# An attention and MLP kernel: token chunks of 512 in place of 384, and the PSUM banks shared out anew

## The chip, the cores and the metric

The kernel runs on one core of one Trainium2 chip. The core has TensorE (PE, matrix products; PEld is its loading of the stationary operand), VectorE (DVE), ScalarE (ACT), GpSimd (POOL) and SyncE (SP), which issues the DMAs. The metric is the device time of one execution in microseconds. Sums of matmuls land in PSUM, which has eight banks of 128 partitions x 512 float32.

## What is computed

Attention over 8 batches, 8 heads, 576 tokens and 64 dimensions a head, with two masks, and then a block over the 512 dimensions of the joined heads:

```
scores = where(mask[h], q @ k.T / 8, -1e9)    # 32 tokens back, or every 4th of 128 back
attn   = exp(scores - max) / (sum + 1e-9)
x      = (attn @ v) joined over heads         # 8 x 576 x 512
u      = x + (x.T @ U @ V).T                  # U: 576 x 32, V: 32 x 576, over the tokens
out    = u + relu(u @ w_ch1) @ w_ch2          # 512 -> 2048 -> 512
```

U and V mix all the tokens of a batch, so no token of a batch can enter the last line before the attention of its whole batch is done. The 8 x 576 = 4608 tokens are 36 tiles of 128.

## The kernel before

**The MLP.** It works on chunks of CT = 3 tiles (384 tokens), 12 chunks. A chunk has 16 steps f, one for each 128 of the 2048 hidden values. Step f of layer 1 (`layer1`) sums 12 matmuls of 384 columns in one PSUM bank (tile `ph`): each product is made of a high and a low part of both operands, as w1h x uth, w1l x uth, w1h x utl, four matmuls each. ACT then writes the high part of the relu (`hh`, L751), and DVE the low part (`hl`, L752), which reads both `ph` and `hh`. Step f of layer 2 (`layer2`) adds, for each token tile, hh x w2h, hh x w2l and hl x w2h, 512 columns each, to the tile's bank (`acc`). At the end of a chunk DVE adds `acc` to x (L788) and SP stores it. The transposed high and low parts of the chunk's tokens, `uth` (ACT, L579) and `utl` (DVE, L580), are made before the chunk begins, from a tile transposed on PE (tiles 0 to 5) or by DVE and DMA (`turn_x`, from tile 6 on).

**The banks.** Three serve attention and the rest (`ps`), three hold `acc`, two hold `ph`.

**Attention.** A batch has nine groups of four units. A unit is a score matmul (`s`), an addition of the mask (L407) and the negated row maximum (L410, `nmax`) on DVE, the exponential on ACT (L414). DVE transposes the group's result in 32 x 32 blocks (L440, L443, eight instructions), PE multiplies by v (`pv`), and DVE normalizes and writes x (L479). From batch 2 on a score's operands are split in a high and a low part first, by ACT (L354) and POOL (L355, L358). When a batch is done, x is multiplied by U (`t`, L519), split (`ts`), multiplied by V (`m`, L543) and added to x (L545).

**What sets the order.** Batch 0 runs first, and in it the weights begin: each piece is read as int64 words and narrowed by ACT, DVE (L210, L214) and POOL, then split (L222, L223). The rest of the weights is emitted through the steps of chunk 0 (`weight_step`, W_RATE a step). The items of batches 1 to 7 stand in a list (`queue`) with a position in chunks; `slot()`, called between groups of the MLP's matmuls, emits the items whose position has come. Batch b runs from position 1.5b - 2.1 to 1.5b - 0.8 (384-token chunks); batch 1 is done at 0.55. What the program emits is put into each engine's order by a scheduler at build time; the engines run their orders as they stand.

Of the kernel before, what the change touches and what calls it, by code (L numbers as in the profile page):

```python
# [10 lines left out]
F32 = mybir.dt.float32  # L11
# [21 lines left out]
HALF_D = DM // 2  # L33
FC = DF // P
NTILE = B * S // P
CT = 3
CTOK = CT * P
NCHUNK = NTILE // CT
UNITS = 4
# [6 lines left out]
NGB = len(TILES) // 2  # L46
# [1 line left out]
DPART = [[NJ - 1]] + [[j, j + 1] for j in range(0, NJ - 1, 2)]  # L48
NU = 9 + len(DPART)
LAG = 2  # L50
MARGIN = 0.3
PRE_AT = range(1, 7)
PRE_N = 6
W_FROM = 11
W_EACH = 3
W_RATE = 4
# [91 lines left out]
def attention_moe_kernel(ctx: ExitStack, tc: tile.TileContext, qk1, qk2, vv, masks, wide, ident, ut, vt, w1, w2, out):  # L148
# [217 lines left out]
    def score(g, u):  # L366
        n = UNITS * g + u
        two = n >= N2 and not is_odd(n)
        if u == 0:
            p_sb = work.tile([P, UNITS, KW], F32, tag="p", name=f"p{g}", bufs=2)  # L370
            pool, n_ = (early, 3) if g < NGB else (work, 2)
            nmax = pool.tile([P, UNITS], F32, tag="nmax", name=f"nmax{g}", bufs=n_)
            ssum = pool.tile([P, UNITS], F32, tag="ssum", name=f"ssum{g}", bufs=n_)
            state[g] = [p_sb, nmax, ssum, None]
        if two:
            sp = psum.tile([P, 2 * KW], F32, tag="ps", name=f"s{g}_{u}")
            split_qk(n)
            t = pairs.pop(n)
            nc.tensor.matmul(sp, lhsT=t[:, 0:P], rhs=t[:, P:], start=True, stop=True)  # L379
# [42 lines left out]
    def turn(g, p_sb):  # L422
        pt = pts[g % NPT]
        if g < PE_T:
            tp = psum.tile([KB, UNITS, P], F32, tag="ph" if g < NGB else "ps", name=f"ptp{g}", bufs=2 if g < NGB else 3)
            for u in range(UNITS):
                nc.tensor.transpose(out=tp[:, u, :], in_=p_sb[:, u, 0:KB], identity=id_sb)
            if g in PT_ACT:
                nc.scalar.copy(out=pt, in_=tp)
            else:  # L430
                nc.vector.tensor_copy(out=pt, in_=tp)  # L431
            return pt
        for r in range(P // WIN):
            rs = slice(WIN * r, WIN * (r + 1))
            for k in (r % 2, r % 2 + 1):
                ks = slice(WIN * k, WIN * (k + 1))
                if is_wide(g):
                    s = r // 2
                    to = pt[ks, 2 * s:2 * s + 2].rearrange("k p (h q) -> k (p h) q", h=2)
                    nc.vector.transpose(out=to[:, :, WIN * (r % 2):WIN * (r % 2 + 1)],  # L440
                                        in_=p_sb[rs, :, QB * s + WIN * k:QB * s + WIN * (k + 1)])
# [45 lines left out]
    t_ps = {}  # L487
# [94 lines left out]
    def batch_items(b):  # L582
# [47 lines left out]
        after = []  # L630
        for c in range(2):
            more = []
            for i in range(n + 1):
                def go(i=i, c=c):
                    if i > 0:
                        t_mm(b, i - 1, c)
# [79 lines left out]
    for b in range(1, B):  # L716
        lo, hi = max(0.0, 1.5 * b - 2 - LO0), 1.5 * b - 0.5
        if b == 1:
            hi = HI1
        its = batch_items(b)  # L720
        queue += [(lo + (hi - MARGIN - lo) * at_, it) for at_, it in its]
    for t in range(DVE_FROM * CT, NTILE):
        done = 1.5 * ((P * t + P - 1) // S) - 0.5 - MARGIN
        at_ = max(t // CT - 1 + TURN_AT + TURN_GAP * (t % CT), done)
        queue.append((at_, lambda t=t: turn_x(t)))
    queue.sort(key=lambda e: e[0])

    for c in range(NCHUNK):
        slots = [0]
        uh, ul = uts.pop(c)  # L730
        acc = [psum.tile([P, DM], F32, tag="acc", name=f"acc{c}_{i}", bufs=3) for i in range(CT)]
        ht = {}

        def slot():
            pos = c + slots[0] / (6 * FC - 3)
# [133 lines left out]
```

## Time and profile before

| | us |
|---|---|
| median of three runs | 1045.84 |
| lowest, highest | 1044.07, 1045.98 |
| the profiled execution | 1044.13 |
| its span, first to last instruction | 1042.3 |

The mean granted clock of PE over the span is 0.972. The page's busy times overlap each other. Rows of instruction groups give the line, engine and operation, output <- input, the count, the busy time, the mean ns of one and the idle time ahead of it. Matmuls are pipelined and their ends are modelled, so what a matmul costs is read from start to start in the timeline. A float32 matmul stands as two rows.

### The profile page before, as it was taken

What the parts mean: (1) busy time and instruction counts of PE and PEld (TensorE: products, weight loads), DVE (VectorE), ACT (ScalarE), POOL (GpSimd) and SP (SyncE); (2) the same over time, 40 slices, a digit from 0 to 9 for tenths busy, and PEclk for the clock granted to TensorE, in tenths of its full rate; (3) what the DMA queues carried; (4) which work ended last, traced back from release to release, by engine and by line L of the source; (5) the groups of instructions that cost most, each with busy time, mean ns of one, the idle gap of its engine ahead of it and who ended that gap; (6) DMA issues with size and microseconds to landing.
All of it is one profiled execution on the core that took longest, in us unless ns stands there. A gap on an engine that the chain in (4) does not pass through costs nothing.

```text
span 1042.3 us, 17400 instructions
## 1 busy us (share of the span) xinstructions
PE 997.2 (96%) x5304; PEld 895.1 (86%) x5304; DVE 669.3 (64%) x2238; ACT 411.3 (39%) x1225; POOL 338.4 (32%) x533
## 2 busy tenths in 40 slices
PE   6679888999999999999999999999999999999997
PEld 6568776898899898999889898999889898999996
DVE  5999998776557863777547873777737874311211
ACT  4646744445233632544324542445324542111110
POOL 1568756434122621425213431325214431000000
PEclk9669899899999999999999999999999999999999
DMA  9656724433232422424232431524233320500000
GB/s 278 190 178 202 234 91 119 111 103 97 73 90 83 127 82 74 117 82 126 82 82 79 120 96 45 138 78 125 74 91 90 104 75 26 130 1 1 31 1 31
DMA packets 97198, 103.06 MB, mean 99 GB/s; under 512 B 12848, under 2 KB 84080, under 8 KB 97104
## 3 DMA queue, kind: packets, MB, share of 16 engines
q1 hardware_dynamic: 97104, 101.94, 34.0%
q8 instruction: 43, 0.70, 0.3%
q14 instruction: 51, 0.42, 0.1%
HBM read 79.86 MB, written 17.30 MB: 93 GB/s over the span
## 4 chain that ended last, share of the span: by engine, by line
PE 81%; DVE 12%; DMA 3%; issue 2%; ACT 1%; SPq 0%; POOL 0%; DVEq 0%; ACTq 0%; POOLq 0%
PE ph L746 36%; PE acc L763 35%; PE pv L451 5%; PE s L379 3%; DVE v L214 2%; PE t L519 2%; DVE pt L443 2%; DVE v L210 1%; DVE utl L580 1%; PE m L543 1%; DMA raw<-ut 1%; DMA raw<-w 1%; DMA raw<-vt 1%; PE s L390 1%; DVE hl L752 1%
## 5 line engine op out<-in xcount | busy, mean ns | idle before, releaser
L763 PE MATMUL acc<-w2h,hh 128*128 128x512 f32 x576 | 229.0, 398 | 4.5 <-ACT hh L751 4.5
L763 PE MATMUL acc<-w2l,hh 128*128 128x512 f32 x576 | 228.1, 396 | 0.0
L355 POOL TENSOR_TENSOR qks<-qkr,qks 128x160 fp32r<-128x160 f32 x192 | 104.1, 542 | 375.4 <-ACT qks L354 262.8
L763 PE MATMUL acc<-w2h,hl 128*128 128x512 f32 x576 | 214.2, 399 | 4.5 <-DVE hl L752 4.4
L752 DVE SCALAR_TENSOR_TENSOR hl<-ph,hh 128x384 fp32r<-128x384 f32 x192 | 105.9, 552 | 166.4 <-ACT hh L751 166.0
L751 ACT ACTIVATE hh<-ph 128x384 fp32r<-128x384 f32 x192 | 93.5, 487 | 280.5 <-PE ph L746 270.7
L414 ACT ACTIVATE p<-p,nmax 128x160 f32<-128x160 f32 (+1 forms) x288 | 117.5, 409 | 155.4 <-DVE nmax L410 153.1
L746 PE MATMUL ph<-uth,w1h 128*128 128x384 f32 x768 | 175.1, 342 | 0.0
L746 PE MATMUL ph<-uth,w1l 128*128 128x384 f32 x768 | 174.6, 340 | 0.0
L746 PE MATMUL ph<-utl,w1h 128*128 128x384 f32 x768 | 173.4, 339 | 0.0
L746 PEld LDWEIGHTS ph<-uth,w1h 128*128 128x128 f32 x768 | 139.3, 190 | 14.7
L746 PEld LDWEIGHTS ph<-uth,w1l 128*128 128x128 f32 x768 | 137.1, 189 | 0.5
L746 PEld LDWEIGHTS ph<-utl,w1h 128*128 128x128 f32 x768 | 135.7, 188 | 1.3
L763 PEld LDWEIGHTS acc<-w2h,hl 128*128 128x128 f32 x576 | 107.9, 189 | 29.0 <-DVE hl L752 7.7
L440 DVE STREAM_TRANSPOSE pt<-p 32x128 f32<-32x128 f32 x384 | 115.9, 302 | 20.3 <-ACT p L414 15.1
L763 PEld LDWEIGHTS acc<-w2h,hh 128*128 128x128 f32 x576 | 108.6, 189 | 20.7 <-ACT hh L751 5.5
L763 PEld LDWEIGHTS acc<-w2l,hh 128*128 128x128 f32 x576 | 108.7, 189 | 14.7
L354 ACT CAST qks<-qkr 128x288 fp32r<-128x288 f32 x192 | 81.8, 431 | 83.3 <-PE s L379 55.7
L358 POOL TENSOR_TENSOR qks<-qkr,qks 64x128 fp32r<-64x128 f32 x192 | 90.2, 470 | 15.0
L407 DVE TENSOR_TENSOR p<-s,wide_sb 128x160 f32<-128x160 f32 x192 | 60.6, 319 | 49.9 <-PE s L379 48.1
L451 PE MATMUL pv<-v,pt 96*128 96x128 f32 x576 | 82.8, 289 | 4.6 <-DVE pt L431 2.6
L451 PEld LDWEIGHTS pv<-v,pt 96*128 96x128 f32 x576 | 79.0, 203 | 9.3 <-DVE pt L431 3.7
(68 smaller groups left out, 1066.1 us busy)
## 6 DMA issues: line engine op xcount, KB each, us to landing
qkr<-qk SPq DMA_DIRECT2D x192, 144.0 KB, 2.2
raw<-w SPq DMA_DIRECT2D x26, 512.0 KB, 4.2
v<-vv SPq DMA_DIRECT2D x126, 96.0 KB, 2.0
out<-x SPq DMA_DIRECT2D x36, 256.0 KB, 2.5
zd<-z SPq DMA_DIRECT2D x120, 64.0 KB, 1.9
xt<-zd SPq DMA_DIRECT2D x30, 256.0 KB, 2.8
qkr<-qk SPq DMA_DIRECT2D x22, 224.0 KB, 4.4
qk<-qk SPq DMA_DIRECT2D x7, 448.0 KB, 7.3
```

The lines of the kernel that those rows point to most:

```text
L354: nc.scalar.copy(out=t[:, 0:QK2], in_=raw)
L355: nc.gpsimd.tensor_tensor(out=t[:, QK2:], in0=raw[:, P:], in1=t[:, P:QK2].bitcast(F32), op=ALU.subtract)
L358: eng.tensor_tensor(out=t[lo, 0:P], in0=raw[lo, 0:P], in1=t[lo, 0:P].bitcast(F32), op=ALU.subtract)
L379: nc.tensor.matmul(sp, lhsT=t[:, 0:P], rhs=t[:, P:], start=True, stop=True)
L407: nc.vector.tensor_tensor(out=p_sb[:, u, :], in0=sp[:, 0:KW], in1=wide_sb[:, kind], op=ALU.add)
L414: nc.scalar.activation(out=p_sb[:, u, 0:w], in_=p_sb[:, u, 0:w], func=AF.Exp, bias=nmax[:, u:u + 1], scale=-1.0, accum_out=ssum[:, u:u + 1],)
L440: nc.vector.transpose(out=to[:, :, WIN * (r % 2):WIN * (r % 2 + 1)], in_=p_sb[rs, :, QB * s + WIN * k:QB * s + WIN * (k + 1)])
L451: nc.tensor.matmul(pv[:, u, :], lhsT=pt[:, u, :], rhs=v_sb[:, u % 2, :], start=True, stop=True)
L746: nc.tensor.matmul(ph, lhsT=w[:, k, :], rhs=u[:, k, :], start=(n == 0), stop=(n == len(seq) - 1))
L751: nc.scalar.activation(out=hh, in_=ph, func=AF.Relu)
L752: nc.vector.scalar_tensor_tensor(out=hl, in0=ph, scalar=0.0, in1=hh.bitcast(F32), op0=ALU.max, op1=ALU.subtract)
L763: nc.tensor.matmul(acc[i], lhsT=h[:, ss], rhs=w, start=(f == 0 and n == 0), stop=(f == FC - 1 and n == 2))
```

## The change

Chunks have CT = 4 tiles, so there are nine. `acc` has four banks, `ph` one, `ps` still three (PSB). Layer 1's matmuls have 512 columns. Batch 1 ends at position 0.70 of the longer chunk, batch 2 runs from 0.82 to 1.60, and batch b from b - 1.45 to b - 0.40. Batch 0's two `t` sums go to an `acc` bank. Tiles 0 to 7 are transposed on PE, as DVE_FROM is still two chunks. Before the MLP five weight steps are emitted in a row, not six; x has 18 buffers, not 16. T_BEHIND is 1, which is what the code did.

```diff
-CT = 3
+CT = 4
+PSB = 3
+B1_END = 0.70
+B2_AT = 0.82
+EARLIER = 0.45
+DONE = 0.40
-MARGIN = 0.3
-PRE_N = 6
+PRE_N = 5
+T_BEHIND = 1
-AHEAD_AT = 0.9
-LO0 = 0.1
+AHEAD_AT = 0.82
-NX = 16
+NX = 18
-HI1 = 0.85
...
-sp = psum.tile([P, UNITS, KB], F32, tag="acc" if g < NGB else "ps", name=f"s{g}", bufs=3)
+sp = psum.tile([P, UNITS, KB], F32, tag="acc" if g < NGB else "ps", name=f"s{g}", bufs=CT if g < NGB else PSB)
...
-tp = psum.tile([KB, UNITS, P], F32, tag="ph" if g < NGB else "ps", name=f"ptp{g}", bufs=2 if g < NGB else 3)
+tp = psum.tile([KB, UNITS, P], F32, tag="ph" if g < NGB else "ps", name=f"ptp{g}", bufs=1 if g < NGB else PSB)
...
-t_ps[b, c] = psum.tile([2 * RANK, HALF_D], F32, tag="ps", name=f"t{b}_{c}")
+t_ps[b, c] = psum.tile([2 * RANK, HALF_D], F32, tag="ps" if b else "acc", name=f"t{b}_{c}", bufs=PSB if b else CT)
...
+def span(b):
+    if b < 2:
+        return 0.0, b * B1_END
+    return (B2_AT if b == 2 else b - 1 - EARLIER), b - DONE
...
-queue = [(HI1 - MARGIN, lambda: ahead(0)), (AHEAD_AT, lambda: ahead(1))]
+queue = [(B1_END, lambda: ahead(0)), (AHEAD_AT, lambda: ahead(1))]
 for b in range(1, B):
-    lo, hi = max(0.0, 1.5 * b - 2 - LO0), 1.5 * b - 0.5
...
+    lo, hi = span(b)
+    queue += [(lo + (hi - lo) * at_, it) for at_, it in batch_items(b)]
...
-acc = [psum.tile([P, DM], F32, tag="acc", name=f"acc{c}_{i}", bufs=3) for i in range(CT)]
+acc = [psum.tile([P, DM], F32, tag="acc", name=f"acc{c}_{i}", bufs=CT) for i in range(CT)]
...
-ph = psum.tile([P, CTOK], F32, tag="ph", name=f"ph{c}_{f}", bufs=2)
+ph = psum.tile([P, CTOK], F32, tag="ph", name=f"ph{c}_{f}", bufs=1)
```

The lines of the changed kernel are numbered a few higher than before's: hl is L758 in place of L752, a layer-1 matmul L752 in place of L746, L407 becomes L410 and L410 becomes L413. The scheduler makes new orders of it. In names, hl0_14 is chunk 0, step 14, and the last number is a running one.

On DVE, at the end of the weights in chunk 0, before (w2h_13 is the last weight block):

```order
L752 SCALAR_TENSOR_TENSOR hl0_14_1869<-ph0_14_1855,hh0_14_1868 128x384
L499 TENSOR_TENSOR xhl1_3_1_1636<-x7_991,xhl1_3_1_1636 128x256
L222 CAST w2h_13_1407<-v_34_1526 128x512
L499 TENSOR_TENSOR xhl1_4_1_1650<-x8_1041,xhl1_4_1_1650 128x256
L529 TENSOR_TENSOR ts1_1_1669<-t1_1_1617,ts1_1_1669 32x256
L545 TENSOR_TENSOR x4_346<-x4_346,m1_0_1_1677 64x256
L752 SCALAR_TENSOR_TENSOR hl0_15_1930<-ph0_15_1891,hh0_15_1929 128x384
```

and in the changed kernel:

```order
L217 SCALAR_TENSOR_TENSOR v_34_1508<-raw34_1_1401,v_34_1508 128x256
L758 SCALAR_TENSOR_TENSOR hl0_8_1703<-ph0_8_1684,hh0_8_1702 128x512
L532 TENSOR_TENSOR ts1_0_1572<-t1_0_1314,ts1_0_1572 32x256
L225 CAST w2h_13_1370<-v_34_1508 128x512
L758 SCALAR_TENSOR_TENSOR hl0_9_1744<-ph0_9_1728,hh0_9_1743 128x512
L548 TENSOR_TENSOR x4_346<-x4_346,m1_0_0_1586 64x256
L548 TENSOR_TENSOR x5_912<-x5_912,m1_1_0_1598 128x256
```

The last weight operation moved from behind hl of step 14 to behind hl of step 8.

On DVE where two chunks meet, before (chunks 4 and 5):

```order
L752 SCALAR_TENSOR_TENSOR hl4_15_5942<-ph4_15_5922,hh4_15_5941 128x384
L545 TENSOR_TENSOR x19_5097<-x19_5097,m4_1_0_5846 128x256
L453 RECIPROCAL ssum44_5701<-ssum44_5701 128x4
L545 TENSOR_TENSOR x20_5195<-x20_5195,m4_2_0_5881 128x256
L752 SCALAR_TENSOR_TENSOR hl5_0_6004<-ph5_0_5980,hh5_0_6003 128x384
L479 TENSOR_TENSOR xp44_5867<-pv44_5860,ssum44_5701 64x2x64 x4
L788 TENSOR_TENSOR x12_2434<-acc4_0_4869,x12_2434 128x512
L788 TENSOR_TENSOR x13_2545<-acc4_1_4870,x13_2545 128x512
L788 TENSOR_TENSOR x14_3549<-acc4_2_4871,x14_3549 128x512
L545 TENSOR_TENSOR x21_5293<-x21_5293,m4_3_0_5896 128x256
L545 TENSOR_TENSOR x22_5404<-x22_5404,m4_4_0_5913 64x256
L752 SCALAR_TENSOR_TENSOR hl5_1_6028<-ph5_1_6012,hh5_1_6027 128x384
```

and in the changed kernel (chunks 3 and 4, from the first addition of `acc` to the fourth utl; three rows of nmax stand between hl3_15 and these, and hl4_0 comes ten rows later):

```order
L794 TENSOR_TENSOR x12_2399<-acc3_0_4925,x12_2399 128x512
L794 TENSOR_TENSOR x13_2495<-acc3_1_4926,x13_2495 128x512
L794 TENSOR_TENSOR x14_3240<-acc3_2_4927,x14_3240 128x512
L794 TENSOR_TENSOR x15_3352<-acc3_3_4928,x15_3352 128x512
L443 STREAM_TRANSPOSE pt0_76<-p46_5662 32x4x32 x8
L482 TENSOR_TENSOR x22_4943<-pv45_5754,ssum45_5561 64x2x64 x2
L482 TENSOR_TENSOR x23_5763<-pv45_5754,ssum45_5561 64x2x64 x2
L410 TENSOR_TENSOR p47_5774<-s47_0_5777,wide_sb_72 128x160
L410 TENSOR_TENSOR p47_5774<-s47_1_5791,wide_sb_72 128x160
L455 TENSOR_SCALAR ssum46_5664<-ssum46_5664 128x4
L583 TENSOR_TENSOR utl4_6116<-xt19_5823,uth4_6115 128x4x128
```

The additions of `acc` stood behind the first hl of the new chunk; they now stand ahead of it, with a group's transposes and the last utl behind them.

On PE, one step of the last chunk, before (layer 1 of step 7, then layer 2 of step 6):

```order
L746 MATMUL ph11_7_11152<-uth11_10944,w1h_6_762 128x384 x4
L746 MATMUL ph11_7_11152<-uth11_10944,w1l_6_763 128x384 x4
L746 MATMUL ph11_7_11152<-utl11_10945,w1h_6_762 128x384 x4
L763 MATMUL acc11_0_10976<-w2h_6_764,hh11_6_11139 128x512
L763 MATMUL acc11_0_10976<-w2l_6_765,hh11_6_11139 128x512
L763 MATMUL acc11_1_10977<-w2h_6_764,hh11_6_11139 128x512
L763 MATMUL acc11_1_10977<-w2l_6_765,hh11_6_11139 128x512
L763 MATMUL acc11_0_10976<-w2h_6_764,hl11_6_11140 128x512
L763 MATMUL acc11_1_10977<-w2h_6_764,hl11_6_11140 128x512
L763 MATMUL acc11_2_10978<-w2h_6_764,hh11_6_11139 128x512
L763 MATMUL acc11_2_10978<-w2l_6_765,hh11_6_11139 128x512
L763 MATMUL acc11_2_10978<-w2h_6_764,hl11_6_11140 128x512
```

and in the changed kernel (layer 1 of step 7, the hl products of step 6, the first hh products of step 7):

```order
L752 MATMUL ph8_7_10290<-uth8_10053,w1h_6_769 128x512 x4
L752 MATMUL ph8_7_10290<-uth8_10053,w1l_6_770 128x512 x4
L752 MATMUL ph8_7_10290<-utl8_10054,w1h_6_769 128x512 x4
L769 MATMUL acc8_0_10095<-w2h_6_771,hl8_6_10275 128x512
L769 MATMUL acc8_1_10096<-w2h_6_771,hl8_6_10275 128x512
L769 MATMUL acc8_2_10097<-w2h_6_771,hl8_6_10275 128x512
L769 MATMUL acc8_3_10098<-w2h_6_771,hl8_6_10275 128x512
L769 MATMUL acc8_0_10095<-w2h_6_771,hh8_7_10303 128x512
L769 MATMUL acc8_0_10095<-w2l_6_772,hh8_7_10303 128x512
L769 MATMUL acc8_1_10096<-w2h_6_771,hh8_7_10303 128x512
L769 MATMUL acc8_1_10096<-w2l_6_772,hh8_7_10303 128x512
L769 MATMUL acc8_2_10097<-w2h_6_771,hh8_7_10303 128x512
```

Layer 2's hh products no longer wait for a step; its hl products still come a step later.

More of the change, by code (lines that the diff above doesn't have):

```diff
@@ L154, in attention_moe_kernel @@
     dram = ctx.enter_context(tc.tile_pool(name="dram", bufs=2, space=bass.MemoryType.DRAM))
-    psum = ctx.enter_context(tc.tile_pool(name="psum", bufs=3, space=bass.MemoryType.PSUM))
+    psum = ctx.enter_context(tc.tile_pool(name="psum", bufs=PSB, space=bass.MemoryType.PSUM))
     held_w = {}
@@ L632, in batch_items, with go @@
             more = []
[L633 to L636, printed above, removed]
+            behind = 1 if b == 0 else T_BEHIND
+            for i in range(n + behind):
+                def go(i=i, c=c, behind=behind):
+                    if i >= behind:
+                        t_mm(b, i - behind, c)
                     if i < n and (b, c) != (0, 1):
@@ L713, in ahead @@
                 fetch(n)
-    queue = [(HI1 - MARGIN, lambda: ahead(0)), (AHEAD_AT, lambda: ahead(1))]
-    for b in range(1, B):
-        lo, hi = max(0.0, 1.5 * b - 2 - LO0), 1.5 * b - 0.5
[L718 to L721, printed above, removed]
+    def span(b):
[3 more added lines that the diff above has]
+    queue = [(B1_END, lambda: ahead(0)), (AHEAD_AT, lambda: ahead(1))]
+    for b in range(1, B):
+        lo, hi = span(b)
+        queue += [(lo + (hi - lo) * at_, it) for at_, it in batch_items(b)]
     for t in range(DVE_FROM * CT, NTILE):
-        done = 1.5 * ((P * t + P - 1) // S) - 0.5 - MARGIN
+        done = span((P * t + P - 1) // S)[1]
         at_ = max(t // CT - 1 + TURN_AT + TURN_GAP * (t % CT), done)
@@ L730, in attention_moe_kernel @@
         uh, ul = uts.pop(c)
-        acc = [psum.tile([P, DM], F32, tag="acc", name=f"acc{c}_{i}", bufs=3) for i in range(CT)]
+        acc = [psum.tile([P, DM], F32, tag="acc", name=f"acc{c}_{i}", bufs=CT) for i in range(CT)]
         ht = {}
         def slot():
-            pos = c + slots[0] / (6 * FC - 3)
+            pos = c + slots[0] / ((CT + 3) * FC - CT - 2)
             slots[0] += 1
```

## Prediction

> **What bounds the kernel now.** I read the page first, then the busy time of every engine by stretch, then the timeline of single steps.
>
> ```profile
> PE 997.2 (96%) x5304; PEld 895.1 (86%) x5304; DVE 669.3 (64%) x2238; ACT 411.3 (39%) x1225; POOL 338.4 (32%) x533
> ...
> PE 81%; DVE 12%; DMA 3%; issue 2%; ACT 1%; SPq 0%; POOL 0%; DVEq 0%; ACTq 0%; POOLq 0%
> ```
>
> TensorE (PE) is busy 96% of the span and carries 81% of the chain; DVE carries 12%. The stretches (length, then busy time of PE, PEld, DVE, ACT, POOL, then the granted PE clock) show where those 12% lie:
>
> ```profile
> 60.00:80.00 20.00, 17.18 (x82) 15.03 (x83) 18.51 (x45) 12.43 (x31) 12.37 (x9) 0.79 0.74 239
> 80.00:100.00 20.00, 19.75 (x117) 17.82 (x116) 19.62 (x37) 13.59 (x34) 16.38 (x12) 1.00 0.60 186
> 100.00:120.00 20.00, 16.42 (x81) 14.92 (x81) 19.57 (x56) 11.88 (x33) 14.33 (x12) 0.83 0.69 218
> 120.00:140.00 20.00, 15.95 (x93) 13.52 (x92) 19.45 (x64) 12.07 (x37) 15.04 (x13) 1.00 0.56 170
> ...
> 160.00:180.00 20.00, 17.01 (x80) 12.76 (x78) 17.24 (x33) 9.37 (x24) 13.97 (x18) 1.00 0.36 102
> ...
> 300.00:400.00 100.00, 99.41 (x550) 90.26 (x548) 70.44 (x267) 43.89 (x138) 39.44 (x74) 1.00 0.31 90
> ```
>
> Two regimes. From 60 to 180 us DVE is busy 17 to 20 us of every 20, PE idles and its clock falls to 0.79 and 0.83: DVE bounds. It narrows the weights and does the attention of batch 1 while chunk 0 of the MLP runs. From 200 us on PE is busy 99.4 of 100 us at clock 1.00 and DVE 70: PE bounds, to the end. A step of the MLP (one f) without attention, on PE, ACT and DVE:
>
> ```profile
> 992.94 0.86 PE L746 MATMUL ph<-uth,w1h 128*128 128x384 f32 x4
> ...
> 995.04 0.40 PE L763 MATMUL acc<-w2h,hh 128*128 128x512 f32 x1
> ...
> 995.24 0.49 ACT L751 ACTIVATE hh<-ph 128x384 fp32r<-128x384 f32 x1 [3.67 <-PE ph L746]
> 995.28 0.40 PE L763 MATMUL acc<-w2l,hh 128*128 128x512 f32 x1
> ...
> 995.77 0.56 DVE L752 SCALAR_TENSOR_TENSOR hl<-ph,hh 128x384 fp32r<-128x384 f32 x1 [3.60 <-ACT hh L751]
> ...
> 997.10 0.86 PE L746 MATMUL ph<-uth,w1h 128*128 128x384 f32 x4
> ```
>
> Layer 1's 12 matmuls of 384 columns take 995.04 - 992.94 = 2.10 us, 0.175 each; layer 2's nine of 512 take 997.10 - 995.04 = 2.06, 0.229 each. A step is 4.16 us, a chunk of 16 is 66.6. The eviction starts 0.20 us after layer 1's last column (995.24), hl follows hh at once (995.77), so a bank of layer 1 is free 1.29 us after its sum is complete when ACT and DVE stand ready.
>
> **Layer 1's matmuls.** 2304 of 384 columns become 1728 of 512, the same columns. 2304 x 0.175 = 403.2 us; 1728 at layer 2's 0.229 = 395.7 us. That is 7.5 us less PE work, and the rest of PE's work is as before. The Trainium skill (TensorE: Matmul & The Clock Gate, "Wait — 56ns, not 53.3ns?") has back-to-back matmuls start N / 2.4 GHz plus 2.5 ns apart; for 384 and 512 columns that would be 162 and 216 ns, shorter than both rows, and would save 576 x 2.5 ns = 1.4 us here; by it alone the sum would end 6 us later.
>
> **Chunk 0.** Its 16 steps now carry four token tiles. If PE had the work ready, it could fill its idle time of the DVE stretch with the fourth tile. The order says it can't. In before DVE comes to the last weight operation (the cast of w2h_13) behind hl of step 14, with one step to go; in the changed kernel behind hl of step 8. All of DVE's weights and all but the last product of batch 1's attention stand ahead of hl of step 9, and with one bank layer 1 of step 10 can't begin before that hl.
>
> ```profile
> 168.01 1.24 DVE L499 TENSOR_TENSOR xhl<-x,xhl 64x256 fp32r<-64x256 f32 x2
> 169.18 0.41 DVE L545 TENSOR_TENSOR x<-x,m 128x256 f32<-128x256 f32 x1
> ...
> 170.06 0.55 DVE L752 SCALAR_TENSOR_TENSOR hl<-ph,hh 128x384 fp32r<-128x384 f32 x1
> ...
> 170.95 1.50 DVE L222 CAST w2h<-v 128x512 fp32r<-128x512 f32 x1
> ```
>
> In before the cast ends at 172.4 us. Of what DVE has done by then, the changed kernel leaves for later: five hl (0.5 each), five additions of L545 (2.0), four xhl (1.24 + 0.63 + 0.50), one group of pv products (1.2, below): 8.1 us. It adds a fourth utl (0.6) and 0.13 us on each of ten hl (128 columns more; 384 take 0.55). So the cast ends near 172.4 - 6.2 = 166.2 and hl of step 9 near 166.9: the same DVE work, no faster. Then PE paces: from layer 1 of step 10 to that of step 15 stand 120 matmuls of 512 (27.5 us) and 25 small ones of attention, t and m. Small ones on before's PE:
>
> ```profile
> 501.32 0.31 PE L379 MATMUL s<-qks 128*128 128x320 f32 x1
> 501.47 0.86 PE L746 MATMUL ph<-uth,w1l 128*128 128x384 f32 x4
> 502.17 1.05 PE L451 MATMUL pv<-v,pt 96*128 96x128 f32 x8
> 502.98 0.36 PE L543 MATMUL m<-ts,vs 128*128 128x256 f32 x1
> ```
>
> A score takes 0.15 us (501.32 to 501.47) and a pv 0.2 (eight rows, two to a matmul, in 0.81); t and m have columns between these. 25 are about 3.5: 31 us in all, so 198.
>
> **Into chunk 1.** DVE's groups, back to back, at before's border of chunks 4 and 5:
>
> ```profile
> 504.85 1.89 DVE L580 TENSOR_TENSOR utl<-xt,uth 128x512 fp32r<-128x512 f32 x3
> 506.65 2.52 DVE L440 STREAM_TRANSPOSE pt<-p 32x128 f32<-32x128 f32 x8
> ...
> 511.25 1.20 DVE L479 TENSOR_TENSOR xp<-pv,ssum 64x128 f32<-64x128 f32 x4
> 512.49 1.89 DVE L788 TENSOR_TENSOR x<-acc,x 128x512 f32<-128x512 f32 x3
> ```
>
> From these: utl 0.63, eight transposes 2.5, four pv products 1.2, an addition to x 0.63. And from the groups of lines (mean ns of one):
>
> ```profile
> L752 DVE SCALAR_TENSOR_TENSOR hl<-ph,hh 128x384 fp32r<-128x384 f32 x192 | 105.9, 552 | 166.4 <-ACT hh L751 166.0
> ...
> L410 DVE CUSTOM_DVE_ANT_0 p<-s,p 128x160 f32<-128x160 f32 x192 | 60.7, 320 | 4.1
> L407 DVE TENSOR_TENSOR p<-s,wide_sb 128x160 f32<-128x160 f32 x192 | 60.6, 319 | 49.9 <-PE s L379 48.1
> ...
> L579 ACT CAST uth<-xt 128x512 fp32r<-128x512 f32 x30 | 16.6, 617 | 13.5 <-PE ph L746 13.5
> ```
>
> An L407 or L410 is 0.3 us; hh with 512 columns I take at 0.6 (the uth row, 617 ns for 512 columns) and hl at 0.69 (552 plus 128 of its own columns).
> Layer 1 of step 15 begins at 198 and ends 2.8 later; 0.2 + 0.6 + 0.7 later hl is out, at 202.3. In the changed order DVE then has, ahead of the last utl of chunk 1: ten L407 and L410 (3.0), two groups of pv products (2.4), sixteen transposes (5.0), four additions to x (2.5), four utl (2.5) and small ones (0.4): 15.8 us, so 218.1. Eight matmuls of chunk 1's first step need no utl and go before (1.9): its start is effectively 216.4. In before it was
>
> ```profile
> 186.87 1.48 PE L746 MATMUL ph<-uth,w1h 128*128 128x384 f32 x4
> 188.15 1.48 PE L746 MATMUL ph<-uth,w1l 128*128 128x384 f32 x4
> ```
>
> 186.87 (at half clock: four matmuls take 1.28 us). So chunk 1 begins 29.5 us later. If DVE were no hindrance here, PE's own rows from step 15 to chunk 1 (28 of 512, 6.4; eight pv and five scores, 2.4; sixteen transposes, about 2.4) would give 209.5, 22.6 later.
>
> **The rest.** Before has eleven chunks left, 11 x 66.6 = 732.6 us of PE; the changed kernel eight of 16 x 24 x 0.229 = 87.9, 703.5 in all. Attention is the same but for two groups done earlier. That is -29.1 us. The tail stays: PE's end, then the last additions to x and the store.
>
> ```profile
> 1032.74 3.73 PE acc L763 x16
> ```
>
> PE ends at 1036.47, and 5.8 us follow; a fourth addition is behind a matmul as the third was.
>
> **One bank.** In a step without attention PE now does layer 1 (2.75), four hl of the step before (0.92), eight hh (1.83). The hh needed is ready 0.8 us after layer 1, covered by the 0.92; the bank is free at about 1.5, covered by 2.75. No wait, with 0.1 and 1.2 us to spare. Before had a whole step to spare. At the start of a chunk no hl stands between, so hh of step 0 costs 0.9 each time.
> With attention it is DVE's queue that decides, since ahead of each hl stand rows of attention, and PE can't pass the bank. Batches now come every chunk, and their dense part lies over the chunk's border. I followed two borders by hand. From chunk 3 to 4, counted from hl of step 14: until hl of step 15 DVE has six L407, three L410, eight transposes, three utl and the wait for ACT's exponentials, 8.6 us, where PE has 6.05 of work: 2.6 of waiting. Then, ahead of the fourth utl, three L410 (0.8), four additions to x (2.5), eight transposes (2.5), pv products (1.2) and three more (0.9), so utl is out 8.2 us later, at 16.8; PE has layer 2's last (0.9), attention (1.2) and the eight matmuls that need no utl (1.9), and stands at 12.6: 4.2 of waiting. Together about 7. From 4 to 5 the utl stands earlier and the sum is 3.4. The borders take these in turn: 1 to 2 near 5, 2 to 3 and 4 to 5 3.4, 3 to 4 and 5 to 6 7, 6 to 7 and 7 to 8 0.9: about 28 us. Before had none of this. Between borders DVE has 6.4 to 6.7 us in a dense step where PE has 6.9 to 7.4, so I charge nothing there.
>
> The remaining edits (buffers of x, batch 0's t in an acc bank, T_BEHIND of 1, one weight step fewer ahead) move no work from or to the path beyond what the orders above show. Two more tiles are transposed on PE and not by DVE and DMA; these eight matmuls are within the 11 us.
>
> **Sum.** 1042.3 + 29.5 - 29.1 + 28 = 1070.7 us of span. The median before is 3.5 over the span (1045.84): 1074. The likeliest time is 1074 us.
>
> **Rivals.** *ACT is late too (20%).* hh stands in ACT's queue behind exponentials that wait for DVE:
>
> ```profile
> ACT p L414 <- DVE nmax L410: 153.1, 116, 4.6
> ```
>
> 116 waits, 1.3 us each. In the changed order an exponential stands right ahead of hh in 42 of the 96 steps of chunks 1 to 6, and hh has 0.1 us to spare beside the attention matmuls next to it. At 0.45 us each that is 19 us: 1093. It speaks against it that such waits overlap the DVE waits already counted.
> A long wait can also cost clock:
>
> ```profile
> 106.13 0.79 PE L763 MATMUL acc<-w2h,hh 128*128 128x512 f32 x1 [3.58 <-ACT hh L751]
> 106.72 0.63 PE L763 MATMUL acc<-w2l,hh 128*128 128x512 f32 x1
> 107.15 0.63 PE L763 MATMUL acc<-w2h,hh 128*128 128x512 f32 x1
> ```
>
> After 3.58 us without work the 512s start 0.43 us apart and not 0.229. The Trainium skill (TensorE: Matmul & The Clock Gate, "HAM oscillation — how this bites in real kernels") says that an idle window over about 3.4 us sends PE back to half clock. The row agrees, and the rule speaks against this change, since a 4.2 us wait now stands at two borders. By the rows each matmul then loses 0.2 us; ten or so at both borders lose 4 us, inside the range.
>
> *The queue does not hold (faster, 20%).* If DVE's work spreads so that the utl and hl are out in time, only the PE terms are left: chunk 1 at 209.5 (+22.6), -29.1, the small waits 2: 1038 of span, 1041.5. If DVE's weights also end 4 us sooner, 1037.5. For it speaks that DVE is busy only 70 of 100 us in the PE stretch. It decides where chunk 1's delay and the waits at the borders together fall below 27 us.
>
> *They cancel (same, 7%).* Chunk 1 at 209.5 and some 6 us of waiting: about 1046. The same comes out if the fourth tile is simply hidden behind DVE and the borders cost what the fewer matmuls bring, so that the change does nothing on balance.
>
> **Numbers.** A measurement of this kernel tells 0.2% (2 us) from no change. Forecast 53%, with ACT 20%: slower 73%; faster 20%; same 7%. The range goes from the faster case without any waiting, 1036, to the ACT case, 1095.
>
> **What would show it.** Right: in the changed trace layer 1 of chunk 1 starts at 210 to 220 us; DVE is 95% busy up to about 166, less after; PE has waits for DVE utl and hl of 2 to 4 us at the borders and a busy share clearly below 99% between 220 and 850; the last two chunks take 88 to 89 us each with PE full; a 512-column matmul of layer 1 starts 0.229 us after the other. Wrong: if chunk 1 starts before 205, if PE waits less than 10 us in all after that, or if the attention-free steps themselves wait for hh.

## The result, and the profile after

The changed kernel takes 1094.1 us (median of 4 runs, 1091.9 to 1097.3) against 1045.0 for the kernel before (4 runs): a ratio of 1.0475, interval 1.0443 to 1.0508. It is slower by 49 us. The forecast was 1074, slower; the range ended at 1095. The profiled execution took 1091.94, its span is 1090.2.

The page of the changed kernel, busy times and the chain:

```profile
PE 1010.2 (93%) x4736; PEld 816.4 (75%) x4736; DVE 654.6 (60%) x2188; ACT 401.3 (37%) x1177; POOL 337.6 (31%) x533
...
PE 70%; DVE 16%; DMA 6%; issue 3%; ACT 2%; POOL 1%; SPq 1%; DVEq 0%; POOLq 0%; ACTq 0%
```

PE's busy share fell from 96% to 93% and its share of the chain from 81 to 70; DVE's, DMA's and issue's shares rose. The stretches, as before: length, then busy time of PE, PEld, DVE, ACT, POOL, then the granted clock.

```profile
60.00:80.00 20.00, 14.35 (x55) 9.95 (x54) 16.55 (x31) 11.91 (x24) 10.47 (x9) 0.68 0.55 177
...
100.00:120.00 20.00, 17.87 (x96) 14.42 (x95) 19.67 (x52) 10.75 (x26) 15.37 (x11) 1.00 0.74 226
120.00:140.00 20.00, 13.66 (x71) 10.61 (x70) 19.48 (x56) 12.06 (x36) 15.86 (x13) 0.94 0.58 184
160.00:180.00 20.00, 16.09 (x69) 13.19 (x70) 13.16 (x32) 7.35 (x18) 13.78 (x18) 0.91 0.24 67
300.00:400.00 100.00, 97.85 (x471) 79.96 (x471) 69.83 (x259) 42.93 (x134) 35.65 (x69) 1.00 0.36 99
500.00:600.00 100.00, 94.53 (x444) 76.85 (x443) 62.72 (x225) 37.25 (x111) 30.63 (x58) 0.97 0.32 90
```

DVE still fills the stretch from 80 to about 160 us (18 to 19.7 of 20), but between 300 and 900 PE now idles: 2.2 of 100 us from 300 on, 5.5 from 500 on, where before's stretch from 300 on had 0.6. Waits by what ended them (the engine's line, what it waited for, sum, count, longest):

```profile
PEld acc L769 <- ACT hh L757: 19.0, 49, 1.9
...
PE pv L454 <- DVE pt L434: 13.0, 7, 4.8
...
PE ph L752 <- ACT uth L582: 10.2, 3, 4.8
...
PE ph L752 <- DVE hl L758: 8.5, 9, 4.0
...
PE acc L769 <- ACT hh L757: 8.1, 10, 1.5
```

Layer 2 waits for hh (49 times at the weight load), layer 1 for the next chunk's uth and for hl, which frees the bank, and pv of the first groups of attention for the transposed weights (9.3 of the 13.0 us before 74 us, in batch 0). From the first layer-1 row of each chunk, start to start (us):

| kernel | chunk 0 starts | chunk 1 starts | chunks 1 to 6 | chunk 7 | chunk 8, to its step 15 |
|---|---|---|---|---|---|
| changed | 74.6 | 227.3 | 109.6, 114.2, 114.4, 113.6, 114.5, 109.4 | 91.5 | 83.9 |

Before started chunk 0 at 65.6 and chunk 1 at 186.9; its chunks of 384 took 76.4 to 82.0 us with attention and 66.7 without.

A ledger from these, against before's. Two banks and no attention cost 88.7 us for a chunk of 512 (measured below) and 66.7 for one of 384. Before's chunks 4 to 6 take 238.5 us for two batches of attention, so a batch costs PE (238.5 - 3 x 66.7) / 2 = 19.2, what little PE waits there included. Before then had 11 x 66.7 + 6 x 19.2 = 848.9 us of work from chunk 1 on and used 1042.3 - 186.9 = 855.4: 6.5 of waits and tail. The changed kernel has 8 x 88.7 + 6 x 19.2 = 824.8 and uses 1090.2 - 227.3 = 862.9: 38.1. So the 47.9 us between the spans are 40.4 until chunk 1, -24.1 of work and +31.6 of waiting.

### The profile page after: what moved, and what is told of

It is laid out like the page before. It is cut to its first block, busy times and chain, and to the rows that moved or that the text cites. A ratio compares the mean times of both kernels' runs of the same rounds, so it can differ in the third digit from the quotient of the medians.

```text
span 1090.2 us, 16072 instructions
## 1 busy us (share of the span) xinstructions
PE 1010.2 (93%) x4736; PEld 816.4 (75%) x4736; DVE 654.6 (60%) x2188; ACT 401.3 (37%) x1177; POOL 337.6 (31%) x533
## 4 chain that ended last, share of the span: by engine, by line
PE 70%; DVE 16%; DMA 6%; issue 3%; ACT 2%; POOL 1%; SPq 1%; DVEq 0%; POOLq 0%; ACTq 0%
PE ph L752 31%; PE acc L769 30%; PE pv L454 4%; DVE pt L443 3%; PE s L382 2%; DVE v L217 2%; PE t L522 2%; DVE x L482 1%; DMA v<-vv 1%; DVE v L213 1%; DMA qkr<-qk 1%; DMA zd<-z 1%; DMA raw<-w 1%; DVE x L794 1%; DVE p L413 1%
## 5 line engine op out<-in xcount | busy, mean ns | idle before, releaser
L758 DVE SCALAR_TENSOR_TENSOR hl<-ph,hh 128x512 fp32r<-128x512 f32 x144 | 99.0, 687 | 241.6 <-ACT hh L757 241.0
L757 ACT ACTIVATE hh<-ph 128x512 fp32r<-128x512 f32 x144 | 85.6, 594 | 334.7 <-PE ph L752 334.3
L752 PE MATMUL ph<-uth,w1h 128*128 128x512 f32 x576 | 160.7, 401 | 18.8 <-ACT uth L582 10.2
L769 PE MATMUL acc<-w2h,hl 128*128 128x512 f32 x576 | 166.5, 397 | 1.6 <-DVE hl L758 1.6
L752 PE MATMUL ph<-utl,w1h 128*128 128x512 f32 x576 | 165.0, 399 | 1.4 <-DVE utl L583 1.3
L752 PE MATMUL ph<-uth,w1l 128*128 128x512 f32 x576 | 161.1, 400 | 0.0
L752 PEld LDWEIGHTS ph<-uth,w1h 128*128 128x128 f32 x576 | 106.2, 190 | 45.2 <-DVE hl L758 12.1
L752 PEld LDWEIGHTS ph<-uth,w1l 128*128 128x128 f32 x576 | 109.7, 191 | 26.2
L752 PEld LDWEIGHTS ph<-utl,w1h 128*128 128x128 f32 x576 | 108.1, 190 | 27.3 <-DVE utl L583 2.3
L454 PE MATMUL pv<-v,pt 96*128 96x128 f32 x576 | 84.8, 292 | 17.7 <-DVE pt L434 13.0
L361 POOL TENSOR_TENSOR qks<-qkr,qks 64x128 fp32r<-64x128 f32 x192 | 88.8, 463 | 15.1
L410 DVE TENSOR_TENSOR p<-s,wide_sb 128x160 f32<-128x160 f32 x192 | 57.3, 317 | 38.7 <-PE s L382 36.9
```

Source lines behind the costliest of these rows:

```text
L361: eng.tensor_tensor(out=t[lo, 0:P], in0=raw[lo, 0:P], in1=t[lo, 0:P].bitcast(F32), op=ALU.subtract)
L410: nc.vector.tensor_tensor(out=p_sb[:, u, :], in0=sp[:, 0:KW], in1=wide_sb[:, kind], op=ALU.add)
L454: nc.tensor.matmul(pv[:, u, :], lhsT=pt[:, u, :], rhs=v_sb[:, u % 2, :], start=True, stop=True)
L752: nc.tensor.matmul(ph, lhsT=w[:, k, :], rhs=u[:, k, :], start=(n == 0), stop=(n == len(seq) - 1))
L757: nc.scalar.activation(out=hh, in_=ph, func=AF.Relu)
L758: nc.vector.scalar_tensor_tensor(out=hl, in0=ph, scalar=0.0, in1=hh.bitcast(F32), op0=ALU.max, op1=ALU.subtract)
```

## The experiments

Twelve kernels were timed, each against the kernel before on the same chip; the intervals are of the ratio to it.

**One bank in the kernel before.**

```diff
-ptp: bufs=2 if g < NGB      -ph: bufs=2
+ptp: bufs=1 if g < NGB      +ph: bufs=1
```

> The kernel before (chunks of 384 tokens, its own order of attention) with one bank under the name ph instead of two, for layer 1's sums and for batch 0's transposed weights; the bank set free is left unused. Theory T (the one bank makes the loss: TensorE has to follow the in-order queues of ScalarE and VectorE at every chunk border and in the dense steps, and batch 0's transposes wait for each other): layer 1 starts at 71 to 76 us instead of 65.6, chunk 1 at 192 to 202 instead of 186.9, a border step is 1 to 4 us longer at most of the 11 borders, and the time is 1070 to 1100 us. Rival R (the loss comes from chunks of 512 tokens and the new places of the attention batches, and the second bank hardly mattered): 1043 to 1055 us.

1097.2 us, ratio 1.0510 (1.0485 to 1.0534): 53 us, as much as the whole change costs. Layer 1 starts at 67.7, only 2 later; chunk 1 at 193.5, 6.6 later; from there to layer 1 of chunk 11's step 15 it takes 890.9 us against 843.6, so 47.3 more. At no border from chunk 1 on does PE wait between the last matmul of layer 2 and layer 1 of the next chunk. The border steps (from layer 1 of step 15 to that of the next chunk's step 0) are 0.3 to 3.3 us longer, 17.7 in all; the rest is spread over the other steps, also in a chunk without attention, which takes 71.1 against 66.7. The timeline of its border, PE and ACT:

```profile
943.88 1.66 ACT L579 CAST uth<-xt 128x512 fp32r<-128x512 f32 x3 [3.17 <-PE ph L746]
...
944.38 0.85 PE L763 MATMUL acc<-w2h,hl 128*128 128x512 f32 x3
...
945.45 0.48 ACT L751 ACTIVATE hh<-ph 128x384 fp32r<-128x384 f32 x1
...
945.98 0.50 PE L763 MATMUL acc<-w2h,hh 128*128 128x512 f32 x1 [0.74 <-ACT hh L751]
...
948.19 0.86 PE L746 MATMUL ph<-uth,w1h 128*128 128x384 f32 x4
...
949.59 0.87 PE L746 MATMUL ph<-utl,w1h 128*128 128x384 f32 x4
950.50 0.49 ACT L751 ACTIVATE hh<-ph 128x384 fp32r<-128x384 f32 x1 [4.57 <-PE ph L746]
...
951.04 0.50 PE L763 MATMUL acc<-w2h,hh 128*128 128x512 f32 x1 [0.58 <-ACT hh L751]
```

Layer 1 of step 15 ends at 944.4. ACT first makes three uth (943.88) and only then hh, which PE needs at once, since with one bank the order uses hh in its own step: 0.74 of waiting. At the next chunk's first step no hl stands in between: 0.58. In the other steps the three hl matmuls (0.69) just fail to cover hh, some 0.2 a step. So theory T holds for the kernel before, except that layer 1 starts earlier than it said.

**The second bank given back to the changed kernel, at the cost of a ps bank.**

```diff
-PSB = 3        -ph, ptp: bufs=1
+PSB = 2        +ph, ptp: bufs=2
```

> The changed kernel with two banks for ph again; the bank is taken from the three of the tag ps (scores, weighted values, transposes, t and m), which has two. Theory T: layer 1 starts at 65 to 69 us instead of 74.6, chunk 1 at 212 to 220 instead of 227.3, border steps are 6.5 to 9 us instead of 7.7 to 13.5, and the time is 1050 to 1070 us, if two ps banks carry the attention; waits of TensorE's score and pv rows for ps banks would be the price, up to 10 us. Rival R: within 8 us of the changed kernel's 1092.

1219.2 us (1.1687, 1.1665 to 1.1710), far outside both. Chunks 1 to 6 take 126 to 139 us, and the border steps 30 to 45:

```profile
PE s L382 <- DVE x L482: 19.1, 7, 3.5
PE m L546 <- ACT ts L537: 17.7, 9, 3.1
PE m L546 <- DVE x L548: 12.2, 14, 2.2
PE s L382 <- POOL qks L361: 12.0, 11, 2.4
```

Scores, weighted values, t and m share ps; with two of them a score or an m waits until DVE has read an earlier pv or m (the rows with x; m's wait for ts is for its input). The run prices the third ps bank, not the second ph bank.

**The second bank, with the fourth tile's sums in the third tile's bank.**

```diff
-acc = [psum.tile(... bufs=CT) for i in range(CT)]     -ph, ptp: bufs=1
+acc = [psum.tile(... bufs=3) for i in range(3)]       +ph, ptp: bufs=2
+acc.append(acc[2])
```

Batch 0's scores and t sums, which use the acc banks before chunk 0, then have three and not four.

> The changed kernel with two ph banks and all three ps banks; the bank comes from layer 2, whose sums for the chunk's fourth tile go into the third tile's bank (so the outputs of these two tiles in each chunk are mixed up; the same matrix products, adds and transfers are issued). It prices the second bank within the chunks of 512 tokens. Theory T (the one bank makes most of the loss, as before_one_bank showed for chunks of 384: 53 us there): border steps 6.5 to 8.5 us, attention-free steps 5.5 us, 1045 to 1065 us. Rival R (in the new order of attention something else holds TensorE, so that a second bank gives little): 1080 to 1095 us.

1098.8 us (1.0515, 1.0487 to 1.0542): nothing comes back, the time lies above the rival's range too, and theory T falls as the only cause. Chunk 1 starts at 221.2, 6.1 earlier than in the changed kernel. Chunk 7 takes 88.7 and not 91.5, so the bank's price without attention is 2.8 us a chunk. But the border steps of chunks 1 to 5 are now 15.0, 20.6, 23.5, 15.8 and 24.4 us, where the changed kernel has 9.2, 10.5, 13.4, 9.6, 13.5: the other steps of a chunk get 3 to 7 us shorter together, its border step 6 to 11 longer. PE at the border of chunks 3 and 4, with SP's load and ScalarE's uth of chunk 4's fourth tile:

```profile
559.18 0.39 PE L770 MATMUL acc<-w2h,hl 128*128 128x512 f32 x1
559.41 0.61 PE L382 MATMUL s<-qks 128*128 128x320 f32 x3
564.92 0.60 PE L382 MATMUL s<-qks 128*128 128x320 f32 x1 [4.90 <-DVE nmax L413]
...
568.17 0.43 SPq L563 DMA_DIRECT2D xt<-zd  x1
...
570.81 0.61 PE L382 MATMUL s<-qks 128*128 128x320 f32 x1 [3.05 <-DVE x L482]
...
570.94 0.62 ACT L582 CAST uth<-xt 128x512 fp32r<-128x512 f32 x1 [2.64 <-DMA xt<-zd]
...
573.67 1.63 PE L753 MATMUL ph<-uth,w1h 128*128 128x512 f32 x3
```

Layer 2 ends at 559.4. Until layer 1 at 573.7 PE has only score and pv rows of the next batch in its queue, and they wait for DVE (4.90 and 3.05 us). But layer 1 could not have begun much earlier without them: each of its first eight matmuls reads the uth of all four tiles, and the fourth ends at 571.56, since its load xt went out only at 568.17.

**Four small edits of the order with one bank.** ptp in the empty acc banks; all four transp ahead of layer 2 of step 14; layer 1 of the next chunk's step 0 ahead of layer 2 of step 15; and ph read by ScalarE alone:

```diff
-ptp: tag="ph" if g < NGB
+ptp: tag="acc" if g < NGB

-for t in more[0:2]: transp(t)
+for t in more: transp(t)

+begin(c + 1); chunks[c + 1].layer1(0)
 layer2(FC - 1)

-nc.scalar.activation(out=hh, in_=ph, func=AF.Relu)
-nc.vector.scalar_tensor_tensor(out=hl, in0=ph, ...)
+nc.scalar.activation(out=hr, in_=ph, func=AF.Relu)
+nc.scalar.copy(out=hh, in_=hr)
+nc.vector.tensor_tensor(out=hl, in0=hr, in1=hh, ...)
```

> The changed kernel, in which batch 0's transposed weights (ptp) use the four acc banks that stand empty before chunk 0, not the one ph bank. Theory T (9 us of the loss are batch 0's transposes waiting for the one bank): layer 1 starts at 65 to 68 us instead of 74.6, step 10 of chunk 0 6 to 9 us earlier than 178.3, and the time is 1083 to 1087 us. Rival (the start is later because of the fourth tile's mixing and transposes, or because the weight casts end as late as before): the start moves by under 3 us, or step 10 doesn't follow it, and the time is 1090 to 1094 us.

1093.9 us (1.0448 to 1.0494). The waits of pv for DVE's pt (L434) fall from 13.0 to 6.1 us, yet layer 1 starts at 77.2, not earlier, and step 10 at 178.3, as in the changed kernel (178.2). Theory T missed, the rival holds: batch 0's transposes do wait for the bank, and it costs nothing.

> The changed kernel with all four transp of the next chunk written ahead of layer 2 of step 14, not two ahead and two behind it. Theory T: at the borders 3 to 4 and 5 to 6, where the step takes 13.4 us, the fourth tile's pair is made earlier and the step shrinks to 9 to 11 us; the other borders by 0 to 1.5 us; in all 3 to 10 us less, 1082 to 1089 us. Rival (the wait there is for the attention's last rows of the batch, whose x tiles the transposes need, so their place in the order says nothing): within 2 us of the changed kernel.

1094.2 us (1.0444 to 1.0494); the borders 3 to 4 and 5 to 6 take 13.4 us still. Theory T missed, the rival holds: the place in the program says nothing there.

> The changed kernel with layer 1 of the next chunk's step 0 written ahead of layer 2 of step 15, so that at a border layer 2 stands between the first two uses of the one bank. Theory T (at each of 8 borders TensorE has nothing to do while the first ph of the chunk is evicted, 1.4 us at the attention-free border 7 to 8 where a step takes 7.7 us in place of 5.6 + 0.7): the border steps 15 to 0 and 0 to 1 together 1 to 2 us shorter, 1078 to 1087 us. Rival (the next chunk's four transposes and their evictions, about 2.8 us on ScalarE alone, then have only layer 2 of step 14 to hide behind, and the wait only moves): 1088 to 1096 us.

1093.8 us (1.0453 to 1.0493). At the attention-free border the three steps 15 to 2 take 6.8 + 5.8 + 6.1 us, 18.7 against 7.7 + 5.6 + 5.6 = 18.9. The wait only moved, as the rival said.

> The changed kernel, in which ScalarE alone reads ph: relu(ph) goes to SBUF in float32 (hr), hh is ScalarE's copy of it, and VectorE makes hl from hr and hh in SBUF, so that the one bank is free without VectorE (144 more ScalarE instructions of about 0.6 us; one x buffer fewer, for space). Theory T1 (what holds the bank is mainly the place of hl in VectorE's queue): the waits of layer 1 for hl, some 20 us, go, the attention-free steps fall from 5.6 to 5.5, and the time is 1070 to 1083 us. Rival T2 (what holds it is ScalarE's in-order queue and hh, and ScalarE gets more to do): layer 2 waits longer for hh, and the time is 1088 to 1105 us.

1108.4 us (1.0602 to 1.0636), so both theories miss, T1 by sign and T2 by size. The mechanism of T1 works where there is no attention: steps of 5.54, chunk 7 in 88.8 us, as with two banks. But chunk 0 takes 161.0 against 152.7, and the border steps of chunks 1 to 5 rise to 15.4, 15.9, 22.1, 14.8, 22.6: the picture of the second bank again.

> Both of the two edits before together: layer 1 carried over the border, and ph freed by ScalarE alone. If both theories hold their gains add up: 1060 to 1075 us. If ScalarE's queue is what holds the bank, no better than the carried version alone: 1080 to 1100 us. In neither case below 1044, since one bank still ties TensorE to one queue.

1108.2 us (1.0604 to 1.0644), the time of the freed version alone and above both ranges.

**What holds the border.** In the changed kernel between chunks 3 and 4, VectorE's z, SP's queue, ScalarE's uth and PE:

```profile
539.24 1.30 DVE L556 STREAM_TRANSPOSE z<-x 128x512 f32<-128x512 f32 x2
...
539.97 2.77 SPq L560 DMA_DIRECT2D zd<-z  x6
...
543.59 1.39 SPq L560 DMA_DIRECT2D zd<-z  x3
...
546.58 0.71 DVE L556 STREAM_TRANSPOSE z<-x 128x512 f32<-128x512 f32 x1 [0.75 <-DMA zd<-z]
...
551.79 8.82 SPq L346 DMA_DIRECT2D qkr<-qk  x6
...
560.72 0.84 SPq L322 DMA_DIRECT2D v<-vv  x2
...
561.61 0.42 SPq L563 DMA_DIRECT2D xt<-zd  x1
...
564.79 0.62 ACT L582 CAST uth<-xt 128x512 fp32r<-128x512 f32 x1 [2.98 <-DMA xt<-zd]
...
565.46 2.07 PE L752 MATMUL ph<-uth,w1h 128*128 128x512 f32 x4 [4.67 <-ACT uth L582]
```

The first row holds z of chunk 4's third and fourth tiles. Each tile is stored in four transfers, so the fourth tile's are the last two of the x6 and the first two of the x3; they have landed when the z of 546.58 starts, which takes the same buffer two tiles on and waited 0.75 us for that. (That z belongs to chunk 5.) The fourth tile's load back, xt, stands on SP's queue behind six loads of q and k (8.82 us, since most wait until POOL has read an earlier load's buffer) and goes out at 561.61, 15 us after the store and 21 after its z, not 14, as the expectation for T3 below has it. uth follows at 564.79, layer 1 at 565.46, after 4.67 us of waiting. From this came theory T2, that the batch ends too late, and T3, that the fourth tile's way is too long. T2 had little ground: the tile lay stored for 15 us.

```diff
-EARLIER = 0.45; DONE = 0.40
+EARLIER = 0.50; DONE = 0.50
```

> after_two_banks_shared_acc (two ph banks, the fourth tile's layer 2 sums in the third tile's bank, two tiles of each chunk mixed up) with every attention batch earlier: EARLIER 0.50 for 0.45 and DONE 0.50 for 0.40, so that the next chunk's last tile is mixed and turned two steps sooner. Theory T2 (two things hold TensorE at a border of the changed kernel, the one bank and a batch that ends too late for the last tile's way through DRAM; with the first removed the second took its place, steps of 15 to 24.5 us): border steps fall to 6 to 11 us, chunks 1 to 5 to 102 to 106 us each, and the time is 1050 to 1068 us. Rival (attention is dense around the border for other reasons, so the wait moves with it): the border steps stay above 13 us and the time above 1085 us.

> The changed kernel (one ph bank, right results) with the same earlier batches, EARLIER 0.50 and DONE 0.50. Theory T2: the borders 3 to 4 and 5 to 6 fall from 13.4 us to 9 to 10, but the bank still holds the others and the dense steps: 1078 to 1090 us, so 20 to 35 us above the shared version with two banks. Rival R (the late end of the batches was all of the loss and the bank costs nothing): within 8 us of the shared version.

1111.0 us with two banks (1.0610 to 1.0671) and 1096.7 with one (1.0470 to 1.0529). T2 falls: with two banks all five borders now take 22 to 24 us, as the rival said, though the fourth tile's z is made 8 to 16 us before layer 1 of step 15. Its load xt goes out only 26 to 34 us after that z, still behind the next batch's loads. With one bank both ranges are missed: the borders 3 to 4 and 5 to 6 take 13.1 and 12.5 us, chunk 1 starts 9 us later (236.4), and from there on the kernel is some 4 us shorter.

```diff
-queue.append((at_, lambda t=t: turn_x(t)))
+if t % CT < CT - 1:
+    queue.append((at_, lambda t=t: turn_x(t)))
```

> The changed kernel (one ph bank), in which each chunk's fourth tile is transposed by four TensorE products (transp without turn_x), not by VectorE and the way through DRAM: no z, zd and xt for it, so one x buffer fewer in the ring of 18 and five transfers fewer on SP's queue per chunk; TensorE gets 4 products of about 0.25 us more per chunk. Theory T3 (besides the one bank, a border is held by the fourth tile, whose xt load stood on SP's queue behind the next batch's loads at 561.6 us, 14 us after its z, and by the ring of x buffers that delays the batch's mixing by several steps): the borders 3 to 4 and 5 to 6 fall from 13.4 us to 9 to 10, the bank keeps the rest: 1076 to 1088 us. Rival (the bank is all that holds the border): within 4 us of the changed kernel's 1092.

> The same edit on after_two_banks_shared_acc (two ph banks, three ps banks, the fourth tile's layer 2 sums in the third tile's bank, two tiles of each chunk mixed up). Theory T3 (both holds are gone): border steps of 6 to 9 us in place of 15 to 24.5, chunks 1 to 5 of 101 to 106 us, 1045 to 1062 us, so 20 to 40 us below the version with one bank, which is the price of the bank in the new order. Rival R (the new order of attention is itself what loses the time, and the second bank gives nothing in it): border steps above 13 us, 1080 to 1100 us.

1138.8 us with one bank (1.0862 to 1.0914) and 1121.4 with two (1.0702 to 1.0762). T3 falls too, and both times lie above the rivals' ranges as well. PE in the one-bank version, between chunks 3 and 4:

```profile
596.39 0.31 PE L382 MATMUL s<-qks 128*128 128x320 f32 x1
600.40 0.63 PE L382 MATMUL s<-qks 128*128 128x320 f32 x1 [3.71 <-POOL qks L361]
...
603.09 0.61 PE L382 MATMUL s<-qks 128*128 128x320 f32 x1 [0.92 <-DVE nmax L413]
603.86 1.09 PE L577 MATMUL tp<-id_sb,x 128*128 128x128 f32 x4 [0.17 <-DVE nmax L413]
...
607.34 1.22 PE L753 MATMUL ph<-uth,w1h 128*128 128x512 f32 x2 [0.42 <-ACT uth L582]
```

The four transposes are cheap (1.09 us), but they stand in PE's queue behind three scores of the next batch, which wait for POOL and DVE, and layer 1 begins 11 us after layer 2's last matmul (596.2). The largest part of the loss, 27 of the 45 us, is in chunk 1, whose border step takes 34.5 us and not 9.2; there the four transposes start 24 us after layer 2's last matmul, behind scores and pv of which several wait, for DVE and POOL above all. The Trainium skill (VectorE: DVE Perf Modes, "Rules for kernel authors") advises TensorE for a 128 x 128 transpose where PSUM will do as its destination. The four products themselves are cheap here, as that advice would have it. The rows put the loss to their place in the queue; the kernel got 45 us slower.

## Why the prediction was right, and 20 us short

**Chunk 0: +29.5 forecast, +40.4 measured.** The chain behind step 10 was sized right: step 10 to step 15 31.3 us (31), step 15 to chunk 1 17.8 (18.4; two of its sums are 0.2 and 0.3 off, since 218.1 - 1.9 is 216.2 and 198 + 11.2 is 209.2). But chunk 1 starts at 227.3, outside the 210 to 220 us that were to show the forecast right: step 10 itself began at 178.2 and not at 166.9. DVE and PE there:

```profile
169.11 0.69 DVE L758 SCALAR_TENSOR_TENSOR hl<-ph,hh 128x512 fp32r<-128x512 f32 x1 [0.20 <-ACT hh L757]
...
170.96 0.43 DVE L225 CAST w2h<-v 128x512 fp32r<-128x512 f32 x1 [0.32 <-POOL v L219]
...
171.47 1.09 PE L752 MATMUL ph<-uth,w1h 128*128 128x512 f32 x4
...
175.15 0.69 DVE L758 SCALAR_TENSOR_TENSOR hl<-ph,hh 128x512 fp32r<-128x512 f32 x1 [3.76 <-ACT hh L757]
...
178.16 1.08 PE L752 MATMUL ph<-uth,w1h 128*128 128x512 f32 x4
```

The failed step is "the cast ends near 172.4 - 6.2 = 166.2": the cast of w2h_13 ends at 171.4. The forecast let DVE work as densely as before, but from 60 to 173 us it is busy 102.6 us and not 108.4, 5.8 less, 2 of them while chunk 0 begins 9.0 us later (the fourth tile's mixing, transposes and evictions stand ahead of it; with ptp out of the bank's way it was no earlier). And hl of step 9 doesn't follow the cast by 0.7 but by 4.4, since layer 1 of step 9 had itself waited for the bank (hl of step 8, 169.11) and began at 171.47; then step 10 begins 2.3 behind hl. These are 5.2 + 3.7 + 2.3 of the 11.3 us. With the second bank step 10 begins at 164.3 and chunk 1 6.1 us earlier.

**The rest: -29.1 forecast, -24.1 measured.** Layer 1's 512 columns start 0.231 us apart, not 0.229, and so do layer 2's; a chunk is 88.7, not 87.9, so eight of them take 6.1 us more than forecast, and before's eleven 1.1 more. Layer 1 itself saves 144 x 12 x (0.175 x 4/3 - 0.231), about 4 us, not 7.5.

**One bank: 28 forecast, 31.6 measured.** The size was nearly right, in part by luck. Followed by hand were the borders 3 to 4 and 4 to 5: about 7 and 3.4; the rows give 13.4 + 8.7 us where the same two steps need 8.1 + 5.9 of work, so 8, and 9.6 + 7.2, so 3. But at 3 to 4 the forecast had 2.6 of waiting for hl and 4.2 for the last utl, both from DVE's queue. In the trace hl costs 0.4 and utl nothing; 4.67 are the wait for the fourth uth, whose load was late on SP's queue, and 2.5 the half clock behind it, a path that the forecast left out. "No wait" in attention-free steps failed, and the prediction had named a wait for hh there as a sign of being wrong: chunk 7's other steps take (91.5 - 7.7) / 15 = 5.59, with two banks 5.54, and the border step 7.7, with two banks 5.6. PE waits twice around the border:

```profile
988.89 2.18 ACT L582 CAST uth<-xt 128x512 fp32r<-128x512 f32 x4 [4.10 <-PE ph L752]
...
989.63 1.09 PE L769 MATMUL acc<-w2h,hl 128*128 128x512 f32 x4
...
990.98 0.59 ACT L757 ACTIVATE hh<-ph 128x512 fp32r<-128x512 f32 x1
...
991.62 0.50 PE L769 MATMUL acc<-w2h,hh 128*128 128x512 f32 x1 [0.90 <-ACT hh L757]
...
996.38 1.09 PE L752 MATMUL ph<-utl,w1h 128*128 128x512 f32 x4
997.51 0.60 ACT L757 ACTIVATE hh<-ph 128x512 fp32r<-128x512 f32 x1 [5.94 <-PE ph L752]
...
998.16 0.50 PE L769 MATMUL acc<-w2h,hh 128*128 128x512 f32 x1 [0.69 <-ACT hh L757]
```

hh of step 15 stood on ScalarE behind the four uth (2.18 us) and came 0.90 late, a place that the forecast didn't count; then 0.69 at step 0, for which it had 0.9. With the steps that is 2.8 a chunk in place of 0.9.

**The cause.** The forecast gave these waits to the bank. The runs bear out half of that. One bank is enough to lose 53 us in the kernel before. But in the changed order the second bank doesn't bring them back: with it, and with ph freed early, chunks 1 to 5 take 112 to 122 us against 88.7 + 19.2 = 107.9 of work. It looks as if two holds stand one behind the other, so that taking away the first shows the second. What the second is, the rows show in part. Before, the last uth of a chunk ends 0.9 to 2.1 us ahead of its layer 1 (chunks 2 to 11). With one bank in the kernel before it is 2.6 to 4.7 us ahead. In the changed kernel and all its versions, layer 1 of chunks 2 to 6 starts only 0.05 to 2.6 us after the last uth, so here that is what it waits for last or nearly so. The new order lays a batch over the chunk's border, and the fourth tile's load (on SP) or its transposes (on PE) stand in their queue behind rows of the next batch that wait for DVE and POOL. That this is the cause is not shown: no run moved that load alone ahead on SP's queue, each edit made a new order of everything, and which part of the change brings it (batches 512 and not 576 tokens apart, the border of four tiles, the number of x buffers) is not settled.

**The rivals.** ACT late (1093, 20%) lies nearest to the time. PE's weight loads do wait 19.0 us for hh, 49 times, the price that it named, but that is chance: it counted 42 steps of chunks 1 to 6, and there (215 to 920 us) only 14 of these waits lie, 5.3 us in all. PE's matmuls wait 8.1 for hh in the whole kernel. So it is a part and not the explanation. The faster rival, that the waits go away, did not come in any stretch: chunk 1 started well after 205, and PE's waits from 215 to 920 us sum to 26. The clock's price came as forecast: after the wait of 4.67 us four matmuls take 2.07 us (row 565.46), elsewhere 1.10; all twelve of that step are slow, 2.5 us, and at the border 5 to 6 another 1.5, together the 4 us that it named and did not add to its sum. The Trainium skill's rule on idle windows (TensorE: Matmul & The Clock Gate, "HAM oscillation — how this bites in real kernels") agrees with that row; the stretch from 500 on runs at 0.97.

## What to carry to other kernels

A buffer that decouples a fast engine from others' in-order queues is worth its bank even where the average load leaves room: count its price in the steps without other load too, since they are many. When a change removes slack in one place and also rearranges the order, price each alone and both together, since their losses need not add. A border followed by hand can give the right size of a loss with the wrong wait in it: name the wait that ends last, and look for it in the trace. Putting the suspect back shows whether something else waits behind it.

## What the runs showed that was not expected

- The third ps bank is worth more than the second ph bank: 1219 against 1099 us with two ph banks each, 120 us for one bank (the second of these has three acc banks and not four).
- SP's queue makes a tile wait for another's buffer: xt went out 15 us after its data was stored, behind six loads that took 8.82 us to issue.
- Four TensorE transposes of 1.09 us, which replace transfers through DRAM, made the kernel 45 us slower; they stood in PE's queue behind rows that waited.
